# Freeing the gelu derivative's DVE operations from program order in the first iteration of a chunked forward-and-backward kernel

## The chip, the cores and the metric

The kernel runs on one core of one Trainium2 chip. A core has five engines that run beside each other: TensorE (PE, matrix products and transposes into PSUM), VectorE (DVE), ScalarE (ACT), GpSimd (POOL) and SyncE (SP, which here only issues transfers). The metric is the device time of one execution in microseconds; less is better. Durations and waits come from one profiled execution.

## The reference

The reference runs a small speech model forward and then backward, from `x` (2 x 16000 x 256), and returns the output and the gradients of all seven inputs. Everything is bfloat16.

```
h  = gelu(conv3(x, w1))[:, ::2]          # 2 x 8000 x 256
f  = gelu(conv3(h, w2))[:, ::2]          # 2 x 4000 x 256
fe = f @ w_f ;  ge = g @ w_g             # g is 2 x 8 x 256
j  = tanh(fe[:, :, None] + ge[:, None])  # 2 x 4000 x 8 x 256
out = j @ w_o
# then the gradients of out, for a given grad_out, by x, w1, w2, g, w_f, w_g, w_o
```

Gelu is the tanh form. Its derivative is needed in the backward half, at both convolutions.

## The kernel before, in words

The 4000 final time steps of each of the two sequences are cut into eight chunks (seven of 512 columns and one of 416), so there are sixteen chunks, G in the code. A chunk carries four rows of `x` for each final step. The main loop (`for n in range(G)`, L783) handles, in iteration n, three things at once:

- the joint part of chunk n (`joint_units`, L623), four pairs of the eight `u`: tanh (`JT`, L316, ACT), its square (`JSQ`, L540, ACT), the product of `grad_out` with `w_o` (L546, PE), the gradient before the tanh (`NGZ`, L548, DVE), its sum over `u` (`ACCN`, L567, POOL), the output (`o_block`, L644 on PE, L646 on ACT), and the gradient of `w_o` (`gwo`, L693, PE). The last needs `JT` transposed (`JR`): by DMA in later chunks, and in chunk 0 by PE transposes and DVE copies (`jr_block`, L618, through L396 and L398);
- the forward half of chunk n + 1: first convolution (`conv_units`, L249), second convolution (`conv2_units`, L283), `fe_units` (L306);
- the backward half of chunk n - 1 (`d1_units`, `d5_units`, `gwf_units`, `gw2_units`, `e_units`).

`weave` (L702) writes one unit of the joint part after the other, and after each a share of the other two (`fill`), by a `ratio`. In iteration 0 there is no backward half and the ratio is 0.28. The forward half of chunk 0 is written before the loop, between groups of filler products (`warm`, L732).

`gelu` (L202) returns two lists of operations. The first makes the value: a square on ACT (`g_sq`), a scalar-tensor-tensor on DVE (L214, `g_s`), a sigmoid on ACT, a product on DVE (`HT` or `FT`). The second makes the derivative: five DVE operations, two tensor-scalar and three tensor-tensor, which leave their result in `G1` or `G2` (the profile shows both as `G`). For chunk 0 all is cut into halves of 512 elements for each partition, and the scratch tiles are called `rows`; from chunk 1 on one operation takes 1024 elements, in `g_sq` and `g_s`.

The first list goes into the queue `later` and the second into the queue `lazy` (L192). `pump` (L195) is called in `weave` after each unit of the joint part, for one or two operations; `later` goes first. Operations run from `later` show in the profile as L198 (chunk 0's second convolution: L291), those from `lazy` as L200, except the scalar-tensor-tensor, L214. `lazy` is opened (`lazy_on`) when the second convolution has been written, and what is left in both queues is written at the end of each iteration. So iteration 0 writes 48 lazy operations: 30 of chunk 0 on DVE (three gelus, two halves, five operations), 15 of chunk 1 on DVE, and three small copies of edge columns on POOL (L262 and L266).

The order in which each engine gets its instructions is not the order of the code. The framework's planner walks a timetable of its own and gives an engine the earliest-written instruction that is ready by that timetable; one that is not ready is passed over by later-written ones. The engine then runs its list strictly in the planned order. `tc.keep_in_program_order(ins)` adds an edge from `ins` to the instruction written just before it on its engine, so that `ins` cannot be planned ahead of that one. Before the change every operation from `lazy` gets such an edge (L200). Operations of the `later` queue have none, but for the scalar-tensor-tensor of the first convolution's second parity from chunk 2 on (`pinned`).

Of the kernel before, what the change touches and what calls it, by code (L numbers as in the profile page):

```python
# [33 lines left out]
def kernel(  # L34
# [30 lines left out]
    def geom(n):  # L65
        b, ci = chunks[n]
        c0 = ci * CW
        return b, ci, c0, min(CW, MQ - c0)

    def blocks(w):  # L70
        return [(o, min(P, w - o)) for o in range(0, w, P)]
# [91 lines left out]
    def window(n):  # L163
        b, ci, c0, W = geom(n)
        lo = c0 - 1 if ci > 0 else 0
        hi = c0 + W if ci == NCH - 1 else c0 + W - 1
        return lo, hi

    def load_x5(n, o, M):
        pin = tc.keep_in_program_order  # L170
        b = chunks[n][0]
        q0 = window(n)[0] + o
        t = x5p.tile([P, 5, D], BF16, name="X5")
        if q0 == 0:
            nc.vector.memset(t[0:1, 0, :], 0.0)
            pin(nc.gpsimd.dma_start(out=t[0:1, 1:5, :], in_=x[b, 0:4, :].rearrange("(o f) d -> o f d", o=1)))
            src = x[b, 3:4, :]
            ap5 = bass.AP(tensor=src.tensor, offset=src.offset, ap=[[4 * D, M - 1], [1, 5 * D]])
            pin(nc.gpsimd.dma_start(out=t[1:M].rearrange("p f d -> p (f d)"), in_=ap5))
        else:  # L180
            src = x[b, 4 * q0 - 1:4 * q0, :]
            ap5 = bass.AP(tensor=src.tensor, offset=src.offset, ap=[[4 * D, M], [1, 5 * D]])
            pin(nc.gpsimd.dma_start(out=t[:M].rearrange("p f d -> p (f d)"), in_=ap5))
        S[n]["X5", o] = t
# [5 lines left out]


    later, lazy = deque(), deque()  # L192
    lazy_on = [False]

    def pump(k):  # L195
        for _ in range(k):
            if later:
                later.popleft()()  # L198
            elif lazy and lazy_on[0]:
                tc.keep_in_program_order(lazy.popleft()())  # L200

    def gelu(xb, W, h, gp, off, kts=((0, KT),), spare=False, pinned=False):  # L202

# [64 lines left out]
    def conv2_units(n):  # L268
        b, ci, c0, W = geom(n)
        st = S[n]  # L270
        HT = st["HT"]
        if n > 0:
            pump(len(later))
        FT = ftp.tile([P, KT, CW], BF16, name="FT")
        G2 = ftp.tile([P, KT, CW], BF16, name="G2")
        st["FT"], st["G2"] = FT, G2
        xb = gel.tile([P, KT, CW], BF16, name="g_x")
        for mt in range(KT):
            ps = ps_f32()
            k = 0  # L280
            for (i, par, off) in ((1, 0, 2), (0, 1, 1), (2, 1, 2)):
                for kt in range(KT):
                    nc.tensor.matmul(ps[:, :W], lhsT=W2[:, i, kt, mt * P:(mt + 1) * P],  # L283
                                     rhs=HT[:, par, kt, off:off + W], start=(k == 0), stop=(k == 5))
                    k += 1
            nc.scalar.copy(out=xb[:, mt, :W], in_=ps[:, :W])
            yield
        first, second = gelu(xb, W, FT, G2, 0, HALVES if n == 0 else ((0, KT),), n == 0)
        if n == 0:
            for f in first:  # L290
                f()  # L291
        else:
            later.extend(first)
        lazy.extend(second)
        lazy_on[0] = True
# [44 lines left out]
    def d1_units(n):  # L340
        b, ci, c0, W = geom(n)
        st = S[n]
        GF = gfp.tile([P, KT, CW + 4], BF16, name="GF")
        st["GF"] = GF
        if ci > 0:
            nc.gpsimd.tensor_copy(out=GF[:, :, 1:2], in_=S[n - 1]["GFh"][:])
        if ci == NCH - 1:
            nc.gpsimd.memset(GF[:, :, 2 + W:3 + W], 0.0)
        for mt in range(KT):
            ps = ps_f32()  # L350
            for kt in range(KT):
                nc.tensor.matmul(ps[:, :W], lhsT=WFT[:, kt, mt * P:(mt + 1) * P], rhs=st["NGFE"][:, kt, :W],
                                 start=(kt == 0), stop=(kt == KT - 1))
            nc.vector.scalar_tensor_tensor(out=GF[:, mt, 2:2 + W], in0=st["G2"][:, mt, :W], scalar=-1.0,
                                           in1=ps[:, :W], op0=ALU.mult, op1=ALU.mult)
            if mt == KT - 1 and ci < NCH - 1:
                st["GFh"] = halo.tile([P, KT, 1], BF16, name="GFh")
                nc.gpsimd.tensor_copy(out=st["GFh"][:], in_=GF[:, :, CW + 1:CW + 2])
            yield
# [40 lines left out]
    def gwf_units(n):  # L400
        b, ci, c0, W = geom(n)
        st = S[n]
        HT, GF, FT, NG = st["HT"], st["GF"], st["FT"], st["NGFE"]
        bl = blocks(W)
        FN = []
        for k in range(0, len(bl), 2):
            t = rowp.tile([P, 8, P], BF16, name="rows")
            srcs, dsts = [], []
            for j, (o, M) in enumerate(bl[k:k + 2]):
                for kt in range(KT):  # L410
                    srcs.append((FT[:, kt, o:o + M], 4 * j + kt, M))
                    srcs.append((NG[:, kt, o:o + M], 4 * j + 2 + kt, M))
                dsts.append((t[:M, 4 * j:4 * j + 4, :], M, 4 * j, 4 * j + 4))
                FN.append((t, 4 * j, M))
            if all(M == P for _, M in bl[k:k + 2]):
                dsts = [(t[:, :, :], P, 0, 8)]
            transposes(srcs, dsts)
            yield
        ps = ps_f32()
        for k, (t, j, M) in enumerate(FN):  # L420
            for dt in range(KT):
                nc.tensor.matmul(ps[:, dt * D:(dt + 1) * D], lhsT=t[:M, j + dt, :],
                                 rhs=t[:M, j + 2:j + 4, :].rearrange("p k d -> p (k d)"),
                                 start=(k == 0 and dt == 0), stop=(k == len(FN) - 1 and dt == KT - 1))
        flush(n, "F", 0, ps[:])
        yield
# [271 lines left out]
    def chain(*gens):  # L698
        for gen in gens:
            yield from gen  # L700
# [82 lines left out]
    for n in range(G):  # L783
        back, fwd = n > 0, n + 1 < G
        conv = conv_units(n + 1) if fwd else iter(())
        parts = []
        if back:
            for (o, M) in blocks(window(n - 1)[1] - window(n - 1)[0]):
                load_x5(n - 1, o, M)
            d1, e, gwf = d1_units(n - 1), e_units(n - 1), gwf_units(n - 1)  # L790
            nfn = (len(blocks(geom(n - 1)[3])) + 1) // 2
            d5, gw2 = d5_units(n - 1), gw2_units(n - 1)
            nhg = KQ
            parts += [islice(conv, 2), islice(d1, 1), islice(conv, 1), d1, islice(conv, 1),
                      islice(gwf, 1), islice(d5, 1), conv, islice(gwf, nfn - 1), islice(d5, 1), islice(gw2, 1),
                      islice(d5, 1), islice(gw2, 1), d5, islice(gw2, nhg - 2), gwf, gw2]
        else:
            parts += [conv, iter([None] * 3)]
        conv2 = conv2_units(n + 1) if fwd else iter(())
        if back:  # L800
            parts += [islice(e, 1), islice(conv2, 1), islice(e, 1), conv2, islice(e, 5)]
        else:
            parts.append(conv2)
            parts.append(iter([None] * 3))
        if fwd:
            parts.append(fe_units(n + 1))
        if back:
            parts.append(e)
        fill = chain(*parts)
        ratio = (0.85 if n > 0 else 0.28) if n + 1 < G else 0.72  # L810
        for up in range(U // 2):
            step = n * (U // 2) + up
            if n + 2 < G:
                load_x(n + 2, (1, 0, 3, 2)[up])
            if step + 1 < len(orderp):
                load_go(*orderp[step + 1])
            for i in range(2):
                if 2 * step + 4 + i < len(order):
                    load_got(*order[2 * step + 4 + i])

            def ahead():
                for i in range(2):
                    if 2 * step + 2 + i < len(order):
                        tanh(*order[2 * step + 2 + i])
                if step + 1 < len(orderp):
                    load_jr(*orderp[step + 1])

            weave(joint_units(n, up, ahead), fill, ratio)
            if up == U // 2 - 1:
                for _ in fill:  # L830
                    pump(2)
                pump(len(later) + len(lazy))
                lazy_on[0] = False
# [35 lines left out]
    n = G - 1  # L869
# [35 lines left out]
```

## Time and profile before

| | |
|---|---|
| median of 3 runs | 854.25 us (853.19 to 855.17) |
| profiled execution | 852.57 us |
| its span, first to last instruction | 850.8 us |
| mean granted TensorE clock | 0.992 |
| PE busy | 821.0 us (96% of the span) |
| PE weight loads | 600.5 us (71%) |
| DVE busy | 628.5 us (74%) |
| ACT busy | 680.5 us (80%) |
| POOL busy | 392.1 us (46%) |

The profiled execution took 1.77 us more than its span and lies 1.68 us below the median. Busy shares are means over the whole span; a stage of 40 us is 5% of it and can have another bound than the rest. A line number stands for the line that recorded the instruction, so L200 stands for all operations run from `lazy`; the tile names (`rows` for chunk 0, `g_sq`, `g_s` later, `G` for the results) tell them apart.

### The profile page before, as it was taken

To read this page: it belongs to the slowest core of one execution; us is meant where nothing else is said; L and a number is where in the kernel's file an instruction comes from. 1 tells how busy PE (TensorE), PEld (TensorE's weight loads), DVE (VectorE), ACT (ScalarE), POOL (GpSimd) and SP (SyncE) were. 2 spreads that over 40 slices of the span, in tenths; PEclk is the share of its full clock that TensorE was granted. 3 is DMA by queue.
4 is the path that set the end of the run, shared out by engine and by line. 5 is a ranking of instruction groups with operands and counts; after the bars stand their busy time and mean duration, and the time that the engine had idled before them with its cause. 6 is when DMAs were issued, how large, how long until landed. Compare 5 with 4: busy or idle time off the path is not lost.

```text
span 850.8 us, 17235 instructions
## 1 busy us (share of the span) xinstructions
PE 821.0 (96%) x6478; PEld 600.5 (71%) x6552; DVE 628.5 (74%) x1190; ACT 680.5 (80%) x1064; POOL 392.1 (46%) x452
## 2 busy tenths in 40 slices
PE   8877999999999999999999999999999999999998
PEld 4444776777767677787767678677777767777876
DVE  4599777687877868777776887767797776868552
ACT  4786989697997969798796969969797896979533
POOL 1144454454444445454554644444553544545650
PEclk9998999999999999999999999999999999999999
DMA  9976999999999999999999999999999999998942
GB/s 187 188 156 148 232 234 187 227 238 203 238 259 215 239 233 235 247 213 243 205 261 210 247 218 244 172 223 267 219 252 204 247 285 201 251 242 193 226 146 90
DMA packets 379280, 185.60 MB, mean 218 GB/s; under 512 B 326786, under 2 KB 362907, under 8 KB 379198
## 3 DMA queue, kind: packets, MB, share of 16 engines
q1 hardware_dynamic: 359550, 115.19, 75.9%
q0 software_dynamic: 19648, 69.32, 26.0%
q8 instruction: 51, 0.84, 0.4%
q14 instruction: 31, 0.25, 0.1%
HBM read 54.43 MB, written 50.34 MB: 123 GB/s over the span
## 4 chain that ended last, share of the span: by engine, by line
PE 56%; ACT 21%; DVE 16%; issue 4%; DMA 2%; POOL 0%; SPq 0%; DVEq 0%; ACTq 0%; POOLq 0%
PE ps L644 8%; PE GWO_ps L693 7%; PE ps L546 7%; ACT JT L316 7%; PE ps L495 7%; PE ps L518 6%; PE ps L454 5%; DVE NGZ L548 5%; PE ps L283 4%; PE pst L396 4%; ACT OUT L646 3%; PE ps L249 3%; ACT JSQ L540 3%; DVE G L200 3%; DVE HT L198 3%
## 5 line engine op out<-in xcount | busy, mean ns | idle before, releaser
L567 POOL TENSOR_TENSOR ACCN<-ACCN,NGZ 128x1024 f32<-128x1024 f32 (+1 forms) x80 | 168.4, 2104 | 126.2 <-DVE NGZ L548 124.2
L540 ACT ACTIVATE JSQ<-JT 128x1024 bf16<-128x1024 bf16 (+1 forms) x128 | 133.2, 1046 | 73.4 <-DVE NGZ L548 72.4
L548 DVE SCALAR_TENSOR_TENSOR NGZ<-JSQ,ps 128x512 bf16<-128x512 bf16 (+1 forms) x256 | 166.0, 668 | 26.9 <-PE ps L546 21.6
L316 ACT ACTIVATE JT<-FE,GE 128x512 bf16<-128x512 f32 (+1 forms) x256 | 170.2, 721 | 0.5
L646 ACT CAST OUT<-ps 128x512 bf16<-128x512 f32 x248 | 145.4, 599 | 16.8 <-PE ps L644 16.7
L644 PE MATMUL ps<-WO,JT 128*128 128x256 bf16 x992 | 149.3, 275 | 9.1 <-DVE NGZ L548 6.2
L546 PE MATMUL ps<-GOT,WOT 128*128 128x512 bf16 (+1 forms) x472 | 135.6, 376 | 5.7 <-DVE JR L398 3.0
L693 PE MATMUL GWO_ps<-GO,JR 128*128 128x256 bf16 x992 | 140.8, 275 | 0.0
L644 PEld LDWEIGHTS <-JT 128*128 128x128 bf16 x992 | 96.0, 98 | 37.9 <-issue 11.0
L693 PEld LDWEIGHTS <-JR 128*128 128x128 bf16 x992 | 95.9, 99 | 18.9 <-issue 1.6
L214 DVE SCALAR_TENSOR_TENSOR g_s<-g_sq,g_x 128x1024 bf16<-128x1024 bf16 (+1 forms) x45 | 58.1, 1291 | 67.9 <-ACT g_sq L198 67.5
L673 POOL DMA_DIRECT2D out_dram<-OUT x64 | 49.6, 774 | 119.1 <-ACT OUT L646 117.2
L495 PE MATMUL ps<-W1T,GH 128*128 128x256 bf16 (+2 forms) x768 | 104.2, 273 | 0.0
L498 ACT CAST GX<-ps 128x512 bf16<-128x512 f32 (+2 forms) x128 | 74.8, 584 | 23.8 <-PE ps L495 19.1
L249 PE MATMUL ps<-XC,W 128*128 128x512 bf16 (+1 forms) x370 | 88.9, 375 | 3.8 <-DMA XC<-in_x_dram 3.4
L518 PE MATMUL ps<-rows,X 128*128 128x256 bf16 (+2 forms) x768 | 92.3, 273 | 0.0
L495 PEld LDWEIGHTS <-GH 128*128 128x128 bf16 (+2 forms) x768 | 75.0, 99 | 12.4 <-issue 0.8
L518 PEld LDWEIGHTS <-X 128*128 128x128 bf16 (+2 forms) x768 | 74.6, 98 | 12.9 <-issue 1.3
L546 PEld LDWEIGHTS <-WOT 128*128 128x128 bf16 x512 | 49.0, 98 | 45.8 <-issue 5.7
L335 DVE TENSOR_TENSOR ACC<-ACC,ps 128x512 f32<-128x512 f32 x84 | 57.3, 682 | 28.8 <-PE ps L454 24.2
L249 PEld LDWEIGHTS <-W 128*128 128x128 bf16 x384 | 37.7, 98 | 41.2 <-issue 4.5
L508 POOL DMA_DIRECT2D out_dram<-GX x60 | 33.7, 561 | 71.9 <-ACT GX L498 67.9
(138 smaller groups left out, 1309.0 us busy)
## 6 DMA issues: line engine op xcount, KB each, us to landing
GO<-in_grad_out_dram SPq DMA_DIRECT2D x56, 512.0 KB, 5.2
out_dram<-OUT POOLq DMA_DIRECT2D x56, 512.0 KB, 5.8
X<-in_x_dram POOLq DMA_DIRECT2D x58, 320.0 KB, 8.6
out_dram<-GX POOLq DMA_DIRECT2D x55, 256.0 KB, 4.9
GO<-in_grad_out_dram SPq DMA_DIRECT2D x8, 384.0 KB, 3.8
out_dram<-OUT POOLq DMA_DIRECT2D x8, 384.0 KB, 4.8
JR<-JT SPq DMA_TRANSPOSE x136, 5.9
GOT<-in_grad_out_dram SPq DMA_TRANSPOSE x128, 5.2
```

The costliest lines, as they stand in the source:

```text
L249: nc.tensor.matmul(ps[:, :W], lhsT=W1[:, i, kt, mt * P:(mt + 1) * P], rhs=st["X", c][:, kt, 16 + sh:16 + sh + W], start=(k == 0), stop=(k ...
L316: nc.scalar.activation(out=JT[:, mt, :W], in_=S[n]["FE"][:, mt, :W], func=ACT.Tanh, bias=GE[:, b, mt, u:u + 1], scale=1.0)
L495: nc.tensor.matmul(ps[:Mx, cj * D:(cj + 1) * D], lhsT=GH[:, par, kt, j:j + Mx], rhs=W1T[:, i, kt, :], start=(k == 0), stop=(k == last))
L498: nc.scalar.copy(out=t[:Mx, 2 * cp:2 * cp + 2, :], in_=ps[:Mx, :])
L518: nc.tensor.matmul(ps[:, dt * D:(dt + 1) * D], lhsT=st["X5", o][:M, i + 2 * par, dt * P:(dt + 1) * P], rhs=t[:M, j + 2 * par:j + 2 * par + ...
L540: nc.scalar.activation(out=JSQ[:, :, :W], in_=JT[:, :, :W], func=ACT.Square)
L546: nc.tensor.matmul(ps[:, :W], lhsT=WOT[:, kt, mt * P:(mt + 1) * P], rhs=GOT[:, kt, :W], start=(kt == 0), stop=(kt == KT - 1))
L548: nc.vector.scalar_tensor_tensor(out=NGZ[:, mt, :W], in0=JSQ[:, mt, :W], scalar=1.0, in1=ps[:, :W], op0=ALU.subtract, op1=ALU.mult, accum_ ...
L567: nc.gpsimd.tensor_tensor(out=out, in0=in0, in1=st["NGZ", u][:, :, :W], op=ALU.add)
L644: nc.tensor.matmul(ps[:M, j * V:(j + 1) * V], lhsT=st["JT", u][:, kt, o:o + M], rhs=WO[:, kt, :], start=(kt == 0), stop=(kt == KT - 1))
L646: nc.scalar.copy(out=OUT[:M, k, :], in_=ps[:M, :])
L693: nc.tensor.matmul(GWO_ps[:, dt, :], lhsT=JR[:M, j, dt, k, :], rhs=GO[:M, k, j * V:(j + 1) * V], start=(n_gwo[0] == 0), stop=(n_gwo[0] == ...
```

## The change

The edge is added only while a new flag, `lazy_pin`, is set. It is set at the head of each iteration to `n > 0`. In iteration 0 the operations from `lazy` are written at the same places in the code as before, but without the edge; from iteration 1 on nothing differs in the code.

```diff
     later, lazy = deque(), deque()
-    lazy_on = [False]
+    lazy_on, lazy_pin = [False], [False]
 
     def pump(k):
         for _ in range(k):
             if later:
                 later.popleft()()
             elif lazy and lazy_on[0]:
-                tc.keep_in_program_order(lazy.popleft()())
+                ins = lazy.popleft()()
+                if lazy_pin[0]:
+                    tc.keep_in_program_order(ins)
@@
         fill = chain(*parts)
+        lazy_pin[0] = n > 0
         ratio = (0.85 if n > 0 else 0.28) if n + 1 < G else 0.72
```

## The prediction

> **What bounds the kernel now.** I read the page first, then the table by stage, then who waits for whom on TensorE, then the timelines of DVE, PE and POOL in the stage that the change touches. The page:
>
> ```profile
> span 850.8 us, 17235 instructions
> ...
> PE   8877999999999999999999999999999999999998
> ...
> DVE  4599777687877868777776887767797776868552
> ...
> PEclk9998999999999999999999999999999999999999
> ```
>
> The digits are busy tenths of 21 us slices. PE shows 9 almost everywhere; the slices below that stand at the start, and there, while PE has 7, DVE has 9. The granted clock (PEclk) has its dips there too. The table by stage cuts that start out; its columns are the stretch, its length, the busy time and count of PE, PEld, DVE, ACT and POOL, then the clock, the DMA share and GB/s.
>
> ```profile
> 24.70:32.70 8.00, 4.58 (x28) 2.20 (x26) 0.03 (x1) 5.67 (x9) 0.00 (x0) 0.99 1.11 202
> ...
> 42.00:66.00 24.00, 16.12 (x117) 10.49 (x118) 22.88 (x46) 20.39 (x30) 12.02 (x10) 0.93 0.71 160
> 66.00:80.50 14.50, 10.77 (x61) 6.48 (x62) 14.50 (x27) 7.18 (x12) 4.75 (x3) 0.76 0.50 134
> 80.50:100.00 19.50, 19.39 (x148) 12.70 (x148) 16.40 (x33) 19.35 (x29) 10.52 (x12) 1.00 1.09 218
> ...
> 400.00:820.00 420.00, 416.78 (x3360) 311.96 (x3396) 314.75 (x591) 343.33 (x539) 210.29 (x245) 1.00 1.05 226
> ```
>
> From 80.5 us on PE is busy all but 0.1 us in 20, and over 99% (416.78 of 420.00 us) from 400 to 820, at clock 1.00, so there PE is the bound. Before that it is not. Between 42.0 and 80.5 us, most of the first iteration of the chunk loop, PE has 26.9 of 38.5 us and DVE 37.4 of 38.5. DVE sets the pace of that stage. Just ahead of it, from 24.7 to 32.7 us, DVE does nothing (0.03 of 8.00 us). Who PE waits for, in and after that stage (total us, times, longest):
>
> ```profile
> PE ps L644 <- DVE NGZ L548: 6.2, 4, 2.5
> PE ps L249 <- DMA XC<-in_x_dram: 3.4, 1, 3.4
> PE ps L546 <- DVE JR L398: 3.0, 2, 2.1
> PE ps L306 <- DVE FT L198: 1.1, 1, 1.1
> PE pst L396 <- DVE JR L398: 0.9, 2, 0.7
> ```
>
> ```profile
> PE ps L644 <- DVE GH L385: 2.1, 8, 0.3
> PE ps L382 <- DVE GF L354: 0.3, 1, 0.3
> PE ps L422 <- DVE rows L398: 0.2, 1, 0.2
> ```
>
> In the first iteration PE waits 11.2 us for DVE (6.2 + 3.0 + 1.1 + 0.9) and 3.4 us for a load. In the remaining 769 us all its listed waits come to 2.6 us. So time that leaves the first iteration is time off the end, as PE has no later slack to hand it back to, and no wait for a load either.
>
> **The change part by part.** It touches 48 queued operations, all run by `pump` in iteration n = 0: 30 half-size ones of chunk 0 (two parities of the first convolution and the second convolution, two halves each, five operations), 15 full-size ones of chunk 1, and three small POOL copies. No instruction, tile or DMA is added or removed. What goes is the edge from each to the instruction written just before it on its engine. So each may be planned as soon as its inputs exist and its engine has nothing earlier-written that is ready. Whether the planner uses that freedom over long distances can be read in this trace:
>
> ```profile
> 31.81 0.59 PE L249 MATMUL ps<-XC,W 128*128 128x512 bf16 x2 [3.42 <-DMA XC<-in_x_dram]
> ...
> 33.52 0.63 PE L693 MATMUL GWO_ps<-GO,JR 128*128 128x256 bf16 x2
> ...
> 36.80 1.04 PE L644 MATMUL ps<-WO,JT 128*128 128x256 bf16 x8
> ```
>
> L693 is the product for GWO, written in the second pair's turn. It runs at 33.52 us, ahead of L644, the output product of the first pair, at 36.80 us. Free work floats over a whole pair. DVE shows the same, and how the pinned ones stand:
>
> ```profile
> 21.71 0.69 DVE L214 SCALAR_TENSOR_TENSOR rows<-rows,g_x 128x512 bf16<-128x512 bf16 x1 [0.93 <-ACT rows L291]
> 22.85 0.69 DVE L214 SCALAR_TENSOR_TENSOR rows<-rows,g_x 128x512 bf16<-128x512 bf16 x1 [0.44 <-ACT rows L291]
> ...
> 24.24 0.43 DVE L291 TENSOR_TENSOR FT<-rows,g_x 128x512 bf16<-128x512 bf16 x1 [0.36 <-ACT rows L291]
> 32.67 0.77 DVE L398 COPY JR<-pst 128x512 bf16<-128x512 bf16 x2 [8.00 <-PE pst L396]
> 33.36 0.68 DVE L548 SCALAR_TENSOR_TENSOR NGZ<-JSQ,ps 128x512 bf16<-128x512 bf16 x1
> ...
> 33.96 0.29 DVE L200 TENSOR_SCALAR rows<-rows 128x512 bf16<-128x512 bf16 x1
> ```
>
> The JR copies at 32.67 us are written after four NGZ operations and run before them. The first pinned operation of chunk 0 (L200, 33.96 us) stands behind the first NGZ, as written, though its inputs were made by 24.67 us at the latest (24.24 + 0.43, the last FT). So, freed, the 30 operations of chunk 0 can go back into the 8.00 us before 32.67 us and into the three gaps of 0.93, 0.44 and 0.36 us ahead of it.
>
> Step 1, their size. The rows of the second half of the gelu's derivative for chunk 0 (minimum, median, maximum in ns):
>
> ```profile
> L200 DVE TENSOR_SCALAR rows<-rows x6: 280/286/2224, 34.0 to 61.1; 128x512 bf16<-128x512 bf16 x6
> L200 DVE TENSOR_SCALAR G<-rows x6: 279/282/289, 34.8 to 61.4; 128x512 bf16<-128x512 bf16 x6
> L200 DVE TENSOR_TENSOR rows<-rows,G x6: 410/415/419, 35.6 to 62.2; 128x512 bf16<-128x512 bf16 x6
> L200 DVE TENSOR_TENSOR G<-rows x6: 408/418/1744, 39.0 to 65.4; 128x512 bf16<-128x512 bf16 x6
> L200 DVE TENSOR_TENSOR rows<-rows,HT x4: 408/420/425, 36.5 to 55.0; 128x512 bf16<-128x512 bf16 x4
> L200 DVE TENSOR_TENSOR rows<-rows,FT x2: 413/414/415, 58.5 to 64.8; 128x512 bf16<-128x512 bf16 x2
> ```
>
> Twelve TENSOR_SCALAR at 0.28 and eighteen TENSOR_TENSOR at 0.415 us make 3.4 + 7.5 = 10.9 us. Starts on DVE lie some 0.08 us closer than durations (32.67 + 0.77 = 33.44 against the next start at 33.36), so 30 of them take 10.9 - 2.4 = 8.5 us of DVE. In the saturated stage they also show three stretched ones: two of 2.22 us and one of 1.74, together 5.2 us over the medians.
>
> Step 2, how much of it finds an idle place. The idle time on DVE is 8.00 + 0.93 + 0.44 + 0.36 = 9.7 us, more than 8.5. But the planner does not see all of it. PE stood 3.42 us at 31.81 us for a load in the middle of a group, with transposes behind it that were ready; the planner would hardly have put them there if it had known. Without that wait the JR copies come at 32.67 - 3.42 = 29.25 us, and the gap that it sees is 29.25 - 24.67 = 4.6 us. With the three small gaps that is 6.3 us. Both ends: 0 (nothing is moved) and 8.5 us (all moved). I take 6.3, as the rows for the load put it nearest there. The other 2.2 us stays in the saturated stage and costs what it did.
>
> What hides the moved work: the gap itself. If the operations land ahead of the FT chain instead, each delays it by at most 0.42 us; but PE would still stand for the load until 31.81 us, so a delay of FT up to 3.4 us costs nothing.
>
> Step 3, the stretched ones. The timelines of DVE and POOL side by side:
>
> ```profile
> 36.86 2.22 DVE L200 TENSOR_SCALAR rows<-rows 128x512 bf16<-128x512 bf16 x1
> ...
> 44.00 0.69 DVE L198 TENSOR_TENSOR HT<-g_s,g_x 128x1024 bf16<-128x1024 bf16 x1 [1.12 <-ACT g_s L198]
> ...
> 51.26 3.14 DVE L214 SCALAR_TENSOR_TENSOR g_s<-g_sq,g_x 128x1024 bf16<-128x1024 bf16 x1
> ...
> 68.90 1.21 DVE L214 SCALAR_TENSOR_TENSOR g_s<-g_sq,g_x 128x1024 bf16<-128x1024 bf16 x1
> ```
>
> ```profile
> 36.69 2.24 POOL L567 TENSOR_TENSOR ACCN<-NGZ 128x1024 f32<-128x1024 bf16 x1 [16.98 <-DVE NGZ L548]
> ...
> 51.14 2.17 POOL L567 TENSOR_TENSOR ACCN<-ACCN,NGZ 128x1024 f32<-128x1024 f32 x1 [1.71 <-DVE NGZ L548]
> ```
>
> An operation of 0.29 us takes 2.22 beside the add on POOL at 36.69, and the scalar-tensor-tensor of chunk 1 takes 3.14 beside the add at 51.14 where it takes 1.21 at 68.90. Each ends about its usual length after the add does (36.69 + 2.24 + 0.29 = 39.22 against 39.08; 51.14 + 2.17 + 1.21 = 54.52 against 54.40). The adds stay, seven for each chunk by the code, and DVE has other operations of this kind queued at those moments (chunk 1's). I therefore take 0 of the 5.2 us: the next operation is caught in its place. Ends: 0 and 5.2. The Trainium skill's page "SBUF — State Buffer", section "Who interferes with whom", has the rule: DVE with two SBUF inputs, or in a two-port mode, and GpSimd hold one shared port exclusively, and issue order decides who blocks for the whole instruction. The trace agrees (2.22 us against 0.29); by that rule the sum is the 6.3 us alone as long as another such operation is next, and 11.5 us if the next ones read PSUM.
>
> Step 4, the 15 operations of chunk 1. They can only start after their HT or FT (44.00 us for the first), in the stage where DVE has no idle time, so moving them forward inside it is an exchange of order: 0 in the sum. They cost if they stand ahead of the chain to FT of chunk 1 (a rival below). The POOL copies that read G follow DVE and free nothing on PE: 0. Slots of the scratch tiles come free sooner; nobody waits for them in the rows above: 0. The PE clock: it stood at 0.76 in 66.0 to 80.5 us, 10.77 us of busy PE, so up to 2.6 us of PE time there would also go; it lies beside the DVE work which sets the pace, so 0 in the sum.
>
> Sum: -6.3 us. PE's 11.2 us of waits for DVE can take it. Against the profiled execution, 852.57 us with a span of 850.8, that is 846.3 and 844.5. That execution lies 1.7 us below the median 854.25 of the runs; the median becomes 848.0 us.
>
> **The rivals.** First, the collisions go too: with the stream thinner, DVE meets the adds with NGZ operations, which do not stretch:
>
> ```profile
> L548 DVE SCALAR_TENSOR_TENSOR NGZ<-JSQ,ps x16: 673/675/680, 33.4 to 77.5; 128x512 bf16<-128x512 bf16 x16
> ```
>
> Sixteen of them last 673 to 680 ns, among all those adds. Then 8.5 + 5.2 = 13.7 us go: 840.5 us. For it, the granted clock would also recover; against it, PE waits only 11.2 us in all for DVE, and ACT is busy 20.39 of 24.00 us from 42 to 66 us, so it would be next.
>
> Second, nothing moves, or it is hidden. If the planner's own times leave no idle DVE before the JR copies, the ready operations keep their order behind earlier-written work: 854.25 us. For it: ahead of 24.67 us DVE is one chained stretch, idle only where it waits for ACT (0.93, 0.44, 0.36). Against it: the 8.00 us. DMA as the real bound later (share 1.05 in 400 to 820) would hide it as well, but PE shows no wait for a load after 82 us.
>
> Third, slower: the freed operations of chunk 1 come between HT and the chain that makes FT of chunk 1. Their size in the end of the stage:
>
> ```profile
> 66.00:82.30 16.30, 11.09 (x14) 0.79 0.54 136
> ```
>
> That is 11.09 us with its stretched ones for 14 of the 15. Ten of the fifteen, those of the first convolution, can come ahead of FT, 7.4 us by share (11.09 x 10 / 15). If they do, FT is that much later, the end of the iteration waits for FT, FE and the first tanh (PE already waits 1.1 us there), and DVE has nothing left to do behind it. It decides from the point where more than 6.3 us of them stand ahead of FT. With eight to ten of them there and one more caught add (1.9 us) the loss is 7.4 + 1.9 - 6.3 = 3.0 us: 857.2 us; somewhat less, 856.0, is the middle of it. For it: free work floats, as shown. Against it: earlier-written work that is ready goes first, and DVE is saturated, so order alone loses nothing until DVE runs dry.
>
> **How the numbers follow.** The forecast (-6.3) gets 0.50, the collision case 0.18, no change 0.10, the slower case 0.22. A measurement of this kernel tells about 0.2%, 1.7 us, from no change. Faster by more is the first two, 0.68; within is 0.10; slower 0.22. The likeliest case alone runs from 845.7 (all 8.5 us) to 852. The range from 840.5 to 857 takes in the rivals and leaves out what lies beyond each end, under 2 in 10, mostly a re-planned later part that turns out worse.
>
> **What would show it.** Right: L200 on tiles `rows` starts before 32 us; DVE in 24.7 to 32.7 us busy 4 to 8 us; PE's waits for NGZ and JR in the first iteration fall from 9.2 us to 3 to 5; the last of them ends near 74 us instead of 80.5; the tail from there to the end as long as before. Step 3 is wrong if fewer adds meet a stretched DVE operation. Step 4 is wrong if PE's wait for FT of chunk 1 grows beyond 1.1 us. What would make it wrong altogether: the L200 group still starting at 34 us, or new waits of PE after 82 us above the 2.6 us, since the planner lays out the rest anew from other moments.

## The result, and the profile after

| | before | changed |
|---|---|---|
| median of the runs | 853.72 us (6 runs) | 843.63 us (6 runs) |
| profiled execution | 852.57 us | 841.67 us |
| span | 850.8 us | 839.9 us |

The ratio is 0.9867, with a 95% interval of 0.9831 to 0.9904, so the change takes 8 to 14 us off; the medians differ by 10.1 us. The forecast was 848.0 us (6.3 us less than before), its range 840.5 to 857. Ratios here and below are taken against the runs of the kernel before that were recorded with each kernel, and leave disturbed runs out, so that a ratio and the plain medians do not always agree to the last microsecond.

The page of the changed kernel, the rows of slices that were read before:

```profile
PE   8978999999999999999999999999999999999998
...
DVE  4797687776778778687876778777688776869552
...
PEclk9999999999999999999999999999999999999999
```

The second DVE slice (21 to 42 us) went from 5 to 7 and PE shows one 7 at the start instead of two. PEclk shows no slice below 9. The same stages as before, in the table by stage (stretch, length, then busy time and count of PE, PEld, DVE, ACT and POOL, clock, DMA share, GB/s):

```profile
24.70:32.70 8.00, 6.37 (x42) 3.37 (x41) 7.24 (x24) 6.91 (x11) 2.14 (x2) 1.00 1.06 194
32.70:42.00 9.30, 9.05 (x66) 5.70 (x66) 5.80 (x14) 9.01 (x15) 2.91 (x2) 1.00 0.99 170
42.00:66.00 24.00, 18.14 (x141) 12.30 (x141) 23.93 (x47) 20.80 (x32) 15.98 (x10) 1.00 1.04 209
66.00:80.50 14.50, 12.82 (x84) 7.83 (x85) 9.34 (x18) 12.70 (x21) 7.22 (x9) 1.00 0.98 229
...
400.00:809.00 409.00, 405.74 (x3263) 303.57 (x3298) 308.72 (x575) 336.46 (x528) 201.51 (x228) 1.00 1.04 225
```

The idle stretch from 24.7 to 32.7 us now has 7.24 us of DVE work where it had 0.03. Behind it, from 32.7 to 42 us, DVE now has idle time (5.80 of 9.30) and ACT is nearly full (9.01). From 42 to 66 us DVE is still full (23.93 of 24.00). The row from 66 to 80.5 us cannot be set against the one before the change, as iteration 0 ends inside it (at 69.27 us, below). PE's clock is 1.00 in all five rows. After 400 us PE is over 99% busy (405.74 of 409.00), as before. What PE waits for, from 24 to 82 us, and from 72 us to the end:

```profile
PE ps L308 <- DVE FT L198: 3.0, 1, 3.0
PE ps L251 <- DMA XC<-in_x_dram: 1.3, 1, 1.3
PE ps L548 <- DVE JR L400: 1.3, 1, 1.3
PE ps L285 <- DVE JR L400: 1.2, 1, 1.2
PE ps L285 <- DVE HT L198: 0.7, 1, 0.7
PE ps L646 <- DVE NGZ L550: 0.5, 1, 0.5
PE pst L398 <- DVE JR L400: 0.5, 2, 0.3
...
PE ps L646 <- DVE JR L400: 0.3, 1, 0.3
```

```profile
PE ps L646 <- DVE GH L387: 2.1, 8, 0.3
PE ps L384 <- DVE GF L356: 0.3, 1, 0.3
PE ps L424 <- DVE rows L400: 0.2, 1, 0.2
```

Its waits for DVE in iteration 0 came down from 11.2 to 7.5 us (3.0 + 1.3 + 1.2 + 0.7 + 0.5 + 0.5 + 0.3). From 72 us on they are the same 2.6 us as before: nothing that was won is handed back. One wait grew, that for FT of chunk 1, from 1.1 to 3.0 us.

A length that does not depend on the start of a run and on its tail is that from the first FE product of chunk 0 on PE to the first product of chunk 2's first convolution. The first and the last row of each fence carry it; before the change:

```profile
24.77 1.03 PE L306 MATMUL ps<-FT,WF 128*128 128x512 bf16 x4
...
50.24 1.86 PE L644 MATMUL ps<-WO,JT 128*128 128x256 bf16 x8 [2.48 <-DVE NGZ L548]
...
80.59 1.46 PE L249 MATMUL ps<-XC,W 128*128 128x512 bf16 x6
```

and after it (the line numbers of the changed file are two higher):

```profile
25.02 1.16 PE L308 MATMUL ps<-FT,WF 128*128 128x512 bf16 x4
...
30.11 0.59 PE L251 MATMUL ps<-XC,W 128*128 128x512 bf16 x2 [1.33 <-DMA XC<-in_x_dram]
...
61.98 0.59 PE L308 MATMUL ps<-FT,WF 128*128 128x512 bf16 x2 [2.97 <-DVE FT L198]
...
69.27 1.46 PE L251 MATMUL ps<-XC,W 128*128 128x512 bf16 x6 [0.34 <-DMA JR<-JT]
```

It was 80.59 - 24.77 = 55.8 us and is 69.27 - 25.02 = 44.3 us. Of these 11.6 us, 2.1 belong to the load of chunk 1, which PE awaited for 3.42 us before and for 1.33 us here; the load's landing differs from run to run (PE awaited it for 2.66 us in the kernel below with only chunk 1 free, which changes nothing ahead of it). From the end of that wait the stage went from 48.8 to 39.2 us, 9.6 us less, and what follows the stage lasts the same: 850.8 - 80.59 = 770.2 and 839.9 - 69.27 = 770.6 us. I call the first length, 55.8 and 44.3 us, the stage below.

Where the freed operations went, on DVE's timeline after the change:

```profile
12.67 0.29 DVE L200 TENSOR_SCALAR rows<-rows 128x512 bf16<-128x512 bf16 x1
...
24.91 0.42 DVE L293 TENSOR_TENSOR FT<-rows,g_x 128x512 bf16<-128x512 bf16 x1
...
29.84 0.42 DVE L200 TENSOR_TENSOR G<-rows 128x512 bf16<-128x512 bf16 x1
...
31.30 0.68 DVE L550 SCALAR_TENSOR_TENSOR NGZ<-JSQ,ps 128x512 bf16<-128x512 bf16 x1
...
37.56 1.23 DVE L216 SCALAR_TENSOR_TENSOR g_s<-g_sq,g_x 128x1024 bf16<-128x1024 bf16 x1 [2.75 <-ACT g_sq L198]
```

The first L200 on `rows` runs at 12.67 us, inside the value half of chunk 0's gelu, and the last at 29.84 us. All 30 are done before the first NGZ at 31.30 us. Fourteen were put ahead of the last half of FT, which now ends at 24.91 + 0.42 = 25.33 us instead of 24.67; PE still stood for the load afterwards, so that cost nothing, as predicted. At 37.56 us there is something new: DVE waits 2.75 us for ACT.

### The profile page after: what moved, and what is told of

It is laid out like the page before. It is cut to its first block, busy times and chain, and to the rows that moved or that the text cites. A ratio compares the mean times of both kernels' runs of the same rounds, so it can differ in the third digit from the quotient of the medians.

```text
span 839.9 us, 17236 instructions
## 1 busy us (share of the span) xinstructions
PE 816.3 (97%) x6478; PEld 598.2 (71%) x6552; DVE 623.0 (74%) x1190; ACT 679.7 (81%) x1064; POOL 394.6 (47%) x452
## 4 chain that ended last, share of the span: by engine, by line
PE 54%; ACT 23%; DVE 15%; issue 5%; DMA 2%; POOL 0%; ACTq 0%; DVEq 0%; POOLq 0%
ACT JT L318 7%; PE GWO_ps L695 7%; PE ps L646 7%; PE ps L548 7%; PE ps L497 6%; PE ps L520 5%; PE ps L456 5%; DVE NGZ L550 5%; PE ps L285 4%; PE pst L398 4%; ACT OUT L648 4%; ACT JSQ L542 3%; PE ps L251 3%; DVE HT L198 3%; DVE G L200 3%
```

## The experiments

Medians are of all runs of a kernel; "stage" is the length defined above, from one profiled execution of each, so it has no interval.

| kernel | median, us | ratio to before (95%) | stage, us |
|---|---|---|---|
| before | 853.7 | | 55.8 |
| changed | 843.6 | 0.9867 (0.9831 to 0.9904) | 44.3 |
| only chunk 0 free | 848.5 | 0.9922 (0.9887 to 0.9957) | 51.0 |
| only chunk 1 free | 854.3 | 0.9991 (0.9962 to 1.0020) | 55.4 |
| chunk 0 written ahead of the loop | 851.5 | 0.9947 (0.9911 to 0.9984) | 48.1 |
| free in all iterations | 859.4 | 1.0049 (1.0017 to 1.0081) | 44.9 |
| before, fillers | 849.6 | 0.9960 (0.9929 to 0.9992) | 51.4 |
| changed, fillers | 846.8 | 0.9896 (0.9860 to 0.9932) | 43.2 |
| only chunk 0 free, fillers | 846.0 | 0.9930 (0.9899 to 0.9961) | 46.1 |
| before, small adds | 846.5 | 0.9910 (0.9876 to 0.9945) | 45.7 |
| changed, small adds | 841.6 | 0.9864 (0.9815 to 0.9913) | 42.4 |
| changed, chunk 1 carried over | 842.3 | 0.9870 (0.9817 to 0.9923) | 42.2 |
| the same, fillers | 842.0 | 0.9845 (0.9790 to 0.9899) | 38.6 |
| before, copies behind NGZ | 850.5 | 0.9959 (0.9917 to 1.0001) | 50.8 |

### Which of the freed operations carry the gain

The edge is made to depend on the chunk that an operation belongs to: in the first kernel only chunk 0's are free, in the second only chunk 1's.

```diff
-                tc.keep_in_program_order(lazy.popleft()())
+                nn, f = lazy.popleft()      # the queue now holds (chunk, operation)
+                ins = f()
+                if nn > 0:                  # second kernel: if nn != 1
+                    tc.keep_in_program_order(ins)
```

> Only the 30 operations of chunk 0 (and its one POOL copy) lose the edge; the 15 of chunk 1 keep it. Theory (idle DVE ahead of the loop takes chunk 0's work): all of the gain, 843 us or a little less, with L200 on rows done by about 30 us. Rival (the freed operations of chunk 1 and the new order inside the stage give half or more): 848 to 850 us. Second rival (the gain of the changed kernel was a load that landed early): 852 to 854 us.

> The other part alone: the 15 operations of chunk 1 and its two POOL copies lose the edge, the 30 of chunk 0 keep it. Theory: no change, 852 to 855 us, since chunk 1's inputs only exist when DVE is already full. Rival: 847 to 849 us, half of the gain or more.

Chunk 0 alone gives a ratio of 0.9922, 6.7 us off; its median of 848.5 us missed the 843 us of the theory and lies in the range of the rival. Chunk 1 alone gives 0.9991, nothing that can be measured, as the theory had it. So chunk 0's 30 operations carry the main part, but not all: the changed kernel is some 5 us below, which is hardly clear of the noise, as the two intervals overlap a little. The two parts alone add up to less than the whole. DVE in the kernel with only chunk 0 free suggests why:

```profile
40.04 1.23 DVE L217 SCALAR_TENSOR_TENSOR g_s<-g_sq,g_x 128x1024 bf16<-128x1024 bf16 x1 [4.42 <-ACT g_sq L198]
...
53.31 0.69 DVE L551 SCALAR_TENSOR_TENSOR NGZ<-JSQ,ps 128x512 bf16<-128x512 bf16 x1 [2.71 <-ACT JSQ L543]
...
55.75 1.43 DVE L201 TENSOR_SCALAR g_sq<-g_sq 128x1024 bf16<-128x1024 bf16 x1
```

With chunk 0's work gone, DVE has idle time in the stage: 4.42 us ahead of 40.04 and 2.71 us ahead of 53.31. The first is of no use to chunk 1, whose operations need the results of the gelu that goes on at 40.04. The second would be: in the changed kernel, six operations of chunk 1 stand between 48.37 and 51.45 us, where here, bound to their written places, none comes before 55.75 us. So chunk 1's freedom has no idle DVE time to use when it comes alone, and some behind chunk 0's. That this makes up all of the 5 us is not shown: in this profile PE's clock was also below 1.00 (0.82, 0.93 and 0.88 in the three stretches from 32.7 to 80.5 us).

### Place or freedom

All edges stay; the 30 operations are written ahead of the loop.

```diff
+    pump(len(lazy))
     for u in range(2):
         tanh(0, u)
```

> All edges as before the change, but the 30 operations of chunk 0 are written ahead of the loop, behind the forward half of chunk 0, so that program order itself puts them behind FT and ahead of the JR copies. Theory: what counts is the place, not the freedom: 842 to 845 us, FT of chunk 0 no later than before (24.67 us). Rival (freedom to fill single gaps is needed): 849 us or more.

The ratio is 0.9947, 4.5 us off: the place gives part of the gain. The expectation of 842 to 845 us missed, and the median of 851.5 us lies in the range of the rival. In its profile the operations start behind FT at 24.85 us, but 13 of the 30 did not fit ahead of the JR copies and stayed in the stage, which is 48.1 us long.

### Freedom in every iteration

```diff
-        lazy_pin[0] = n > 0
+        lazy_pin[0] = False
```

> No edge in any iteration. From iteration 1 on DVE has slack (14.3 of 19.5 us busy) and PE is over 99% busy, so there is little to win there: the theory expects 843 to 853 us, slower than the changed kernel through NGZ queued behind freed operations. Rival (freedom is good everywhere): below 842 us.

It is slower than the kernel before (1.0049) and some 15 us slower than the changed one, more than the 843 to 853 us that were expected. Its stage is as good, 44.9 us. The loss lies later: what follows the stage lasts 855.4 - 70.39 = 785.0 us instead of 770.6. Two of PE's waits after 82 us:

```profile
PE ps L548 <- DVE ACC L337: 3.4, 10, 0.3
PE ps L285 <- DVE ACC L337: 2.6, 9, 0.3
```

ACC is the sum of weight gradients on DVE. In the changed kernel PE never waits for it after 72 us; with every edge gone it waits 6.0 us in all. That is a part of the 15 us only; the rest does not stand among PE's listed waits, and its cause stays open. The edges earn their place from iteration 1 on.

### What the stretched operations cost

Six of the seven POOL adds of chunk 0 are cut to 8 columns in each half, in the kernel before and in the changed one. Most of the sum over `u` of chunk 0 is left out, and the gradients from it are not the reference's.

```diff
+        if n == 0:
+            if u < U - 1:
+                nc.gpsimd.tensor_tensor(out=st["ACCN"][:, :, :8], in0=st["NGZ", u - 1][:, :, :8],
+                                        in1=st["NGZ", u][:, :, :8], op=ALU.add)
+                return
+            in0 = st["NGZ", u - 1][:, :, :W]
```

> The kernel before with six of the seven POOL adds of chunk 0 cut to 8 columns of 512 in each half; it leaves out most of the sum over u for chunk 0, so the gradients from that chunk are not the reference's. Five of the DVE operations of iteration 0 that last 1.7 to 3.1 us then fall to their usual 0.3 to 1.2 us, some 9 us of DVE. Theory A (DVE sets the pace): 845 to 848 us. If the stretched operations lie beside other work: 852 to 854 us.

> The changed kernel with six of the seven POOL adds of chunk 0 cut to 8 columns of 512 in each half (the gradients from chunk 0 are then not the reference's). In the changed kernel four DVE operations beside those adds are still stretched, by some 5 us together. Theory (DVE still sets the pace of iteration 0): 838 to 841 us. Rival (the stage is now bound by the chain through ACT and PE): 842 to 844 us.

In the kernel before the ratio is 0.9910, 7.7 us off (median 846.5, as theory A had it), and the stage is 10 us shorter: DVE did set the pace there, and the stretched operations cost about as much as the whole of chunk 0's work. PE's wait for NGZ ahead of the output products fell from 6.2 to 1.5 us, that for JR ahead of L546 (3.0 us) is gone, and that for FT grew:

```profile
PE ps L306 <- DVE FT L198: 2.4, 1, 2.4
PE ps L650 <- DVE NGZ L548: 1.5, 5, 0.6
```

In the changed kernel the same cut gives 0.9864 against 0.9867, no difference that can be measured, though the intervals leave room for some 5 us either way. Its stage is 1.9 us shorter in the one profile (42.4 against 44.3). DVE is no longer full there (22.18 of 24.00 us from 42 to 66 us), and waits 4.4 us for ACT ahead of g_s at 41.93 us, instead of 2.75. That stands with the rival, by which the rest of the stretching lies beside other work, but does not settle it; the median (841.6) is between the two expectations.

### When DVE starts, and the PE clock

PE's clock was below 1.00 in iteration 0 of the kernel before and not in the changed one. Ten filler products were put on PE behind the first FE products, so that it would not stand for the load, in three kernels.

```diff
-    for _ in chain(warm(16), ..., warm(16), fe_units(0)):
+    for _ in chain(warm(16), ..., warm(16), fe_units(0), warm(10)):
```

> The kernel before with ten more filler products (2.2 us) on PE between the first FE products and the products of grad_out with w_o, so that PE does not stand long for the load of chunk 1 and its clock need not fall there. Theory A (DVE sets the pace of iteration 0, and the lost clock lies in its shade): 852 to 854 us, the waits of PE for DVE longer by what the clock gives back. Theory B (the clock itself was half of the gain): 847 to 850 us.

> The changed kernel with the same ten filler products. Both theories: its clock was 1.00 in the profiled run already, so the profiled stage does not shorten; fillers may delay it by up to 1 us: 842 to 845 us. The runs above 844 us should become fewer if those were runs in which the clock fell.

> Only chunk 0's operations freed, with the same ten filler products. Theory B (what this version lacked against the changed kernel, 5 us, was the clock, which fell in its profiled run after a wait of 2.0 us for the load): 843 to 845 us. Theory C (it lacked the freedom of chunk 1's operations, which pinned fill DVE at the end of the iteration): 847 to 849 us.

The kernel before has a ratio of 0.9960 with them (3.4 us off; median 849.6, in the range of theory B), which looked like the clock. But its clock was still 0.93 from 42 to 66 us, and on DVE another thing had moved:

```profile
29.60 0.69 DVE L548 SCALAR_TENSOR_TENSOR NGZ<-JSQ,ps 128x512 bf16<-128x512 bf16 x1 [5.24 <-ACT JSQ L540]
```

The planner had now put the first NGZ ahead of the JR copies, so DVE began at 29.60 us and not at 32.67. To tell the two apart, the last experiment takes the fillers out and only binds the copies of the first pair behind what is written ahead of them:

```diff
+        evict = (lambda **kw: tc.keep_in_program_order(nc.vector.tensor_copy(**kw))) if up == 0 else None
-        transposes(srcs, [...])
+        transposes(srcs, [...], evict)
```

> The kernel before, without fillers, with one thing changed: the JR copies of the first pair of chunk 0 are bound behind what is written ahead of them on DVE, so the first NGZ (whose inputs exist at 30 us) no longer stand behind copies that wait for the load of chunk 1. PE still stands for that load, and its clock may fall there. Theory A (the moment at which DVE starts on iteration 0 sets its end): DVE starts near 30 us instead of 32.7, and the time is 849 to 852 us, close to the 849.5 us of the kernel with fillers. Theory B (the fillers helped through the clock): no change, 853 to 855 us.

It has the same time as with fillers (0.9959, median 850.5; the interval just reaches 1), the same stage (50.8 against 51.4 us), and DVE starts at the same point:

```profile
28.93 0.69 DVE L548 SCALAR_TENSOR_TENSOR NGZ<-JSQ,ps 128x512 bf16<-128x512 bf16 x1 [5.24 <-ACT JSQ L540]
```

So in both kernels a start of DVE that is 3 to 4 us earlier goes with 4 to 5 us of stage and some 3.5 us of time, as theory A has it. The times alone do not exclude the clock, for in this profile it was higher too: 1.00, 1.00 and 0.88 in the three stretches from 32.7 to 80.5 us, against 0.82, 0.93 and 0.76 in the kernel before. What speaks for theory A is DVE itself:

```profile
42.00:66.00 24.00, 15.52 (x111) 10.11 (x112) 24.00 (x49) 16.82 (x26) 10.92 (x9) 1.00 0.89 198
```

It is busy 24.00 of 24.00 us here and 14.50 of 14.50 us in the next stretch, and as much in the kernel with fillers, so in these stretches DVE had no idle time that a faster PE could have saved. A run in which the clock alone changes is not among these.

The changed kernel gains nothing from fillers (0.9896; its median of 846.8 us lies above the 842 to 845 us expected), and its runs above 844 us did not become fewer. The clock in iteration 0 need not be what makes such runs long: the profiled executions of "before, fillers" (858.4 us), "changed, small adds" (851.3) and "only chunk 0 free, fillers" (850.9) took 5 to 10 us more than the medians, and in them PE waits 7.6, 6.3 and 3.8 us for transfers (JR, in the first also GOT) after 90 us; it has no such wait in the profiles of the kernel before and the changed one. With only chunk 0 free, fillers shorten the stage of the profiled execution by 4.9 us, but the ratio (0.9930 against 0.9922) does not move, and the median of 846.0 us lies between the two theories; what part the clock has in the 5 us that this kernel lacks stays open.

### Taking chunk 1's operations out of iteration 0

They are left in the queue at the end of iteration 0 and written first in iteration 1, with the edge; a second kernel has the fillers too. The queue holds pairs of chunk and operation, as in the first experiment.

```diff
-            if later:
+            left = lazy and lazy[0][0] == 1 and lazy_upto[0] > 1
+            if later and not left:
                 later.popleft()()
-            elif lazy and lazy_on[0]:
+            elif lazy and (left or lazy_on[0]) and lazy[0][0] <= lazy_upto[0]:
@@
         lazy_pin[0] = n > 0
+        lazy_upto[0] = G if n > 0 else 0
```

> The changed kernel, with the 15 operations of chunk 1 and the two POOL copies behind them carried over into iteration 1, where they are written first, one or two for each unit, with the edge. Theory (what DVE is relieved of in iteration 0 is time off the end as long as PE waits for DVE there, 7.5 us in the changed kernel): 838 to 841 us, and PE's wait for FT of chunk 1 below 1.5 us. Rival (in iteration 1 they delay the value half of the gelu of chunk 2 and NGZ, and the time comes back there): 842 to 847 us.

> The same with ten filler products on PE between the first FE products and the products of grad_out with w_o: as the run before it or up to 1 us faster, with fewer runs far above the median if those are runs in which the PE clock fell at the load of chunk 1.

PE's wait for FT of chunk 1 fell from 3.0 to 0.9 us, and a new one of 1.5 us, for GH of chunk 0, came up in iteration 1.

By ratio the first is where the changed kernel is (0.9870), and its median of 842.3 us lies in the range of the rival. Its stage is 2.0 us shorter, but what follows the stage lasts 1.6 us longer (839.6 - 67.35 against 839.9 - 69.27): most of it comes back. The one with fillers has the shortest stage of all, 38.6 us, the lowest ratio, 0.9845, and a profiled span of 837.5 us; but its interval (0.9790 to 0.9899) holds the changed kernel's ratio, so that it beats it is not shown. Of its stage, too, a part comes back: what follows lasts 3.3 us longer (837.5 - 63.58). Three of its six runs are above 844 us, so these did not become fewer either.

## Why the prediction was right, and where it was off

**The bound.** Right. DVE sets the pace of iteration 0: taking work from DVE there (chunk 0's operations, small adds) or starting DVE sooner (the copies behind NGZ, whose interval just reaches 1) each shortened the kernel, and what the change won came off the end. The size is less well met: 843.6 us lies outside the 845.7 to 852 us of the likeliest case and inside the range only because that takes in the first rival.

**Step 1, 8.5 us in 30 operations.** Right: they all moved, and all of it left the stretch in which DVE is full.

**Step 2, 6.3 us of it finds an idle place.** Too small by 2.2 us: 8.5 us did. The gap between FT and the JR copies that the planner sees, 4.6 us, is borne out: with chunk 0 written ahead of the loop, it put 17 of the 30 operations there, which by the sums of step 1 are 8 x 0.28 + 9 x 0.415 - 17 x 0.08 = 4.6 us. Mis-sized was the place ahead of it. In the changed kernel the planner put 14 of the operations ahead of the last half of FT, more than the 1.7 us of the three small gaps hold, and the 0.7 us by which FT then ended later (25.33 against 24.67) was covered by the wait for the load. The cover was predicted; that it would be used was not.

**Step 3, 0 of the stretched operations.** This is the step that failed, and the term that was most mis-sized. The other stretched rows of the kernel before:

```profile
47.37 2.22 DVE L200 TENSOR_SCALAR rows<-rows 128x512 bf16<-128x512 bf16 x1
...
59.48 1.74 DVE L200 TENSOR_TENSOR G<-rows 128x512 bf16<-128x512 bf16 x1
...
62.50 2.35 DVE L200 TENSOR_SCALAR g_sq<-g_sq 128x1024 bf16<-128x1024 bf16 x1
...
71.85 2.35 DVE L200 TENSOR_SCALAR g_sq<-g_sq 128x1024 bf16<-128x1024 bf16 x1
...
79.09 2.27 DVE L200 TENSOR_TENSOR g_sq<-g_sq,FT 128x1024 bf16<-128x1024 bf16 x1
```

With the two that the prediction showed there are seven, which last 12.6 us longer than usual (1.94, 1.94, 1.92, 1.32, 1.93, 1.93, 1.59). After the change there are five:

```profile
43.35 2.23 DVE L216 SCALAR_TENSOR_TENSOR g_s<-g_sq,g_x 128x1024 bf16<-128x1024 bf16 x1
...
46.50 1.36 DVE L200 TENSOR_SCALAR G<-g_s 128x1024 bf16<-128x1024 bf16 x1
...
55.21 2.57 DVE L200 TENSOR_TENSOR g_sq<-g_sq,HT 128x1024 bf16<-128x1024 bf16 x1
...
62.45 1.76 DVE L200 TENSOR_SCALAR G<-g_s 128x1024 bf16<-128x1024 bf16 x1
...
65.67 2.28 DVE L200 TENSOR_TENSOR g_sq<-g_sq,FT 128x1024 bf16<-128x1024 bf16 x1
```

They last 1.01 + 0.94 + 1.89 + 1.34 + 1.60 = 6.8 us longer than usual, 5.8 us less. The argument was that the adds stay, so the next operation of that kind is caught in place of one that moved. The adds do stay, but POOL now runs them at other moments:

```profile
33.90 2.12 POOL L569 TENSOR_TENSOR ACCN<-NGZ 128x1024 f32<-128x1024 bf16 x1 [4.03 <-DVE NGZ L550]
...
42.37 5.19 POOL L569 TENSOR_TENSOR ACCN<-ACCN,NGZ 128x1024 f32<-128x1024 f32 x2 [2.80 <-DVE NGZ L550]
...
52.90 4.33 POOL L569 TENSOR_TENSOR ACCN<-ACCN,NGZ 128x1024 f32<-128x1024 f32 x2 [3.09 <-DVE NGZ L550]
```

The first runs beside JR copies of usual length (1.08 us for three at 33.73) and then beside DVE's idle time. Four more of the seven come as two pairs (x2), each of which begins while DVE runs NGZ, which do not stretch. That is the first rival's mechanism, and on DVE also its price (5.8 us against the 5.2 of the rival, which counted chunk 0's three rows alone). It is also the prediction's own sign that step 3 is wrong: fewer stretched operations beside the adds. The Trainium skill's rule on the shared port ("SBUF — State Buffer", "Who interferes with whom") gave 6.3 us if another such operation stands next and 11.5 if the next ones read PSUM; the measured stage lies between them, nearer to the second (9.6 us from the end of the load's wait).

**Step 4, chunk 1 at 0.** Right for chunk 1 alone (0.9991), too low in company, by some 5 us that are hardly clear of the noise: freed behind chunk 0's, its operations can fill idle DVE time that only exists since chunk 0's are gone. A sum of parts could not show that. The third rival's condition came true: all ten operations of the first convolution stand ahead of FT of chunk 1, where five stood before, and PE's wait for it grew from 1.1 to 3.0 us, the prediction's sign that step 4 is wrong. But the rival's loss did not come; its price was an estimate from 14 operations taken as 15 (7.4 us; with 14 it is 11.09 x 10 / 14 = 7.9). That the freeing made this wait longer is not shown: it is 2.4 us with chunk 1's operations bound (only chunk 0 free) and 2.8 us with all of them bound (copies behind NGZ). Without them in iteration 0 it is 0.9 us.

**The PE clock at 0.** By the stage rows of the kernel before, PE lost 8.91 x 0.18 + 16.12 x 0.07 + 10.77 x 0.24 = 5.3 us to it from 32.7 to 80.5 us; the changed kernel lost none. Set beside the fall of PE's waits (3.7 us) that adds up to the 9.6 us of the stage within 0.6 us. This is bookkeeping on PE and does not tell cause from effect. That DVE was full in these stretches (22.88 of 24.00 and 14.50 of 14.50 us) speaks for 0; whether the clock gives something of its own was not separated.

**What did not add up to a full gain.** DVE was relieved of 8.5 + 5.8 = 14.3 us and the stage is 9.6 to 11.6 us shorter. About half of the rest is idle time on DVE, which in the stage now waits 2.75 and 0.72 us for ACT (ahead of 37.56 and 39.96 us), against 1.12 us before. ACT is busy 9.01 of 9.30 us there; it is the next limit that the first rival named. The other half was not followed. So the time came out between the forecast (848.0) and the first rival (840.5).

## What to carry to other kernels

Where one engine sets the pace of a short stage, look for idle time on it just ahead of the stage, and for work whose inputs exist by then: moving it there, or starting the stage's own work sooner, is time off the end. An edge that keeps work in written order can be right in the steady part (here worth some 15 us) and wrong in the first pass, so ask for each pass what the engine has to do when the work becomes ready. Parts of a change that are worth nothing alone may be worth something once another part has made room (here some 5 us, hardly clear of the noise), so test them together as well as apart.

## What the runs showed of the hardware

The wait of PE for the load of chunk 1 and what the clock then did do not go together simply. In the kernel before, the clock was 0.50 from 50 to 52 us, behind a wait of 2.48 us (the PE row at 50.24 above), and 0.82 behind the load:

```profile
32.70:42.00 9.30, 8.91 (x53) 5.53 (x53) 9.23 (x24) 6.56 (x12) 2.24 (x1) 0.82 0.83 140
50.00:52.00 2.00, 1.76 (x9) 1.23 (x9) 2.00 (x7) 0.79 (x2) 0.86 (x1) 0.50 0.77 166
```

With only chunk 0 free, the clock fell behind a wait of 2.03 us:

```profile
30.91 0.59 PE L252 MATMUL ps<-XC,W 128*128 128x512 bf16 x2 [2.03 <-DMA XC<-in_x_dram]
```

```profile
32.70:42.00 9.30, 9.08 (x49) 5.08 (x48) 4.15 (x12) 6.97 (x13) 2.85 (x2) 0.82 0.72 137
```

With the copies behind NGZ, a longer wait left it at 1.00:

```profile
29.90 0.59 PE L249 MATMUL ps<-XC,W 128*128 128x512 bf16 x2 [2.48 <-DMA XC<-in_x_dram]
```

```profile
32.70:42.00 9.30, 8.65 (x66) 5.71 (x65) 9.11 (x21) 9.06 (x15) 2.59 (x2) 1.00 1.08 150
```

In the changed kernel a wait of 2.97 us (61.98) also left it at 1.00. In the changed kernel with small adds, on the other hand, it fell behind a wait of 1.71 us for the load (until 32.80 us; clock 0.56 from 34 to 36 us). The Trainium skill's page "TensorE: Matmul & The Clock Gate", section "What's actually happening", has the clock fall to half after an idle window of some 3.4 us that runs freely. The runs agree that the length of a wait alone does not decide, but here the clock fell behind single waits of 1.7 to 2.5 us, shorter than that window. What else decides is not shown.
